# A second level of the seven-product scheme for three of the seven products of an expert's first layer

## The chip, the cores and the metric

The kernel runs on one core of a Trainium2 chip. TensorE (PE) multiplies: a weight load brings in a stationary 128x128 block, and a matmul streams up to 512 columns past it and adds the result up in a bank of PSUM. PSUM has eight banks of 128x512 fp32. VectorE (DVE) and ScalarE (ACT) read and write PSUM and SBUF; GpSimd (POOL) works on SBUF here. SyncE (SP) starts the transfers from and to memory. Each engine runs its own instructions in order and waits for the others by semaphores. The metric is the device time of one execution, in microseconds (us).

## The reference, cut to what matters

```python
x = attention(q, k, v)              # (1152, 512): pooled attention plus attention in a band
# first mixture of experts: 8 experts, P from a softmax and 8 rounds of scaling rows and columns
for e in range(8):
    h = np.maximum(x @ w1[e], 0.0)  # (1152, 512) @ (512, 1024)
    out += P[:, e:e + 1] * (h @ w2[e])          # (1152, 1024) @ (1024, 512)
# second mixture: x is the first one's result; 4 experts, p from an input
for e in range(4):
    h = np.maximum(x @ w1[e], 0.0)
    out += p[:, e:e + 1] * (h @ w2[e])
```

All in fp32. The kernel splits every fp32 operand into a high part and the rest, and makes each product of three matmuls: high by high, high by rest, rest by high.

## The kernel before, in words

The 12 experts run one after the other, each in two groups of 512 hidden columns. A group has two stages. In the first (`quarter_products`, L409, with its matmuls in `product`, L380, on line L396) x times w1 gives the hidden columns; in the second (`tile_products`, L449, matmuls on L455) they are multiplied by w2 for nine tiles of 128 tokens, 12 matmuls of 512 columns each, and `accumulate` (L468) adds the weighted tile to the sum `acc`.

The first stage works on quads: 256 hidden columns of an expert, as 2x2 blocks of 256x128, against x in 2x2 blocks of 576 tokens by 256 inputs. Instead of the eight block products of such a 2x2 product it makes seven, in the order 1, 5, 6, 2, 7, 3, 4, out of sums of blocks (Winograd's form of Strassen's scheme). Every product is done for two halves u of the tokens, 288 columns each: six matmuls (two blocks of 128 inputs, three parts each) into one bank. So a quad is 84 matmuls and a group, with its two quads q, 168. Two groups do without the scheme (`plain_unit`, L372, matmuls on L277): the first of expert 0 and the first of the second mixture, since the sums of x are still being made.

The sums of x (`x_sums`, L866) are made once for each mixture and kept in `sh` and `sl`. The sums of weights are made for each quad (`quad`, L319): POOL subtracts blocks (L327), ACT copies the high part (L301), POOL takes the rest (L303). The results stand in a ring of 12 slots `w1s`, each one block pair for one quad; the raw weights in two buffers `raw1`. The w2 blocks are split in the same way (ring `w2s`). The products come together outside PE: a product is copied from its bank into a `tmp` buffer by ACT (L294), added to a bank's content by DVE into a `tmp` (L406) or to another `tmp` by POOL (L421); other products go on in the bank of an earlier one by PE's own addition. `hidden` (L360) takes the finished block: ACT applies max(.,0) and writes the high part to `ht` (L364), DVE writes the rest (L366), from the bank or from `tmp`.

The order of all instructions is written out beforehand by a planner (`Plan`, L79). It takes the tasks with their assumed durations, walks through time, and gives each engine at each step the task that can begin first, among the next 160 (400 in the attention part) in order of their due times; a due time is the PE clock at which the task was added. Buffers come from rings (`Ring`, L30), in the order in which the program asked for them; a task whose buffer is not free cannot begin. The lists so made are fixed in the program. There are two plans: the attention with the start of expert 0, and all the rest. The scaling rounds of P (`gate_round`, L1023) are mixed into the start of the second plan.

## Time and profile before

| | us |
|---|---|
| median of 3 runs | 1202.19 (1201.57 to 1202.4) |
| the profiled execution | 1204.05 |
| its span, first to last instruction | 1202.3 |
| PE busy in the span | 1191.3 |
| POOL, DVE, ACT busy | 674.2, 664.4, 460.7 |

A line of groups names line, engine, operation, written and read tiles, shape and count; then the busy time of all, the mean of one in ns, and the idle time of the engine ahead of them with what ended it. Matmuls overlap: the duration of one (about 293 ns at 288 columns) is not the time from one to the next, which the chain shows (168 in 22.13 us). A line of the chain has start, length, and what ran. A line of windows has the stretch, its length, and busy time and instructions of PE, PEld (weight loads), DVE, ACT and POOL in it, then the granted clock, DMA share and GB/s.

### The profile page before, as it was taken

The numbers are of one execution on the slowest core, as the hardware profiler recorded it, in microseconds if no ns is written. First come the engines' busy times: TensorE is split into PE (matmuls) and PEld (weight loads), VectorE is DVE, ScalarE is ACT, GpSimd is POOL, SyncE is SP. The second block draws the span as 40 slices with busy tenths as digits, with TensorE's granted clock in tenths as the row PEclk, the third lists the DMA queues.
The fourth block names the chain that finished last, engine by engine and source line by source line (L and its number), as shares of the span: only waits on it lengthen the run. The fifth ranks groups of instructions, "written<-read, shape, count | busy, mean of one in ns | idle before, by whom it ended". The sixth has DMA issues, their size and how long they took to land.

```text
span 1202.3 us, 20145 instructions
## 1 busy us (share of the span) xinstructions
PE 1191.3 (99%) x7800; PEld 1076.9 (90%) x7800; DVE 664.4 (55%) x1208; ACT 460.7 (38%) x1163; POOL 674.2 (56%) x779
## 2 busy tenths in 40 slices
PE   8999999999999999999999999999999999999998
PEld 6889898988989989989989989889899898898997
DVE  6867844635636536546446456367364563653643
ACT  4755451522513514414325325244453252351430
POOL 7968844835836736637538448256384483573620
PEclk9999999999999999999999999999999999999999
DMA  8521210211211201102102112011021121120102
GB/s 215 166 71 36 71 45 27 71 36 36 71 35 36 71 6 66 55 17 71 44 27 71 36 36 71 36 54 35 19 71 37 34 71 36 35 71 22 32 1 79
DMA packets 27344, 63.72 MB, mean 53 GB/s; under 512 B 4528, under 2 KB 5296, under 8 KB 27248
## 3 DMA queue, kind: packets, MB, share of 16 engines
q1 hardware_dynamic: 27248, 62.44, 16.7%
q8 instruction: 61, 1.00, 0.3%
q14 instruction: 35, 0.29, 0.1%
HBM read 60.07 MB, written 2.36 MB: 52 GB/s over the span
## 4 chain that ended last, share of the span: by engine, by line
PE 96%; DMA 1%; POOL 1%; DVE 0%; issue 0%; ACT 0%; SPq 0%; POOLq 0%; DVEq 0%; ACTq 0%
PE bank L455 49%; PE bank L396 40%; PE bank L277 4%; DMA v<-in_v_dram 1%; PE bank L609 0%; PE bank L769 0%; DMA qk<-in_qk_dram 0%; PE bank L931 0%; PE bank L907 0%; PE bank L759 0%; PE bank L734 0%; PE bank L677 0%; PE bank L725 0%; DVE ht L366 0%; POOL t L661 0%
## 5 line engine op out<-in xcount | busy, mean ns | idle before, releaser
L455 PE MATMUL bank<-w2s,ht 128*128 128x512 f32 (+1 forms) x2604 | 595.9, 389 | 0.0
L455 PEld LDWEIGHTS bank<-w2s,ht 128*128 128x128 f32 x2604 | 484.8, 188 | 98.4
L303 POOL TENSOR_TENSOR w2s<-raw,w2s 128x512 fp32r<-128x512 f32 x96 | 132.7, 1392 | 391.1 <-PE bank L455 354.4
L483 DVE SCALAR_TENSOR_TENSOR acc<-bank,prob,acc 128x512 f32<-128x512 f32 (+1 forms) x190 | 142.1, 748 | 323.1 <-PE bank L455 323.1
L396 PE MATMUL bank<-sh,w1s 128*128 128x288 f32 x1408 | 292.8, 294 | 1.4 <-DVE tmp L406 1.4
L396 PEld LDWEIGHTS bank<-sh,w1s 128*128 128x128 f32 x1408 | 229.3, 188 | 1.7 <-DVE tmp L406 1.7
L396 PE MATMUL bank<-xh,w1s 128*128 128x288 f32 x1056 | 226.8, 295 | 0.1
L366 DVE SCALAR_TENSOR_TENSOR ht<-tmp,ht 128x288 fp32r<-128x288 f32 x264 | 216.7, 847 | 4.9 <-ACT ht L364 2.9
L406 DVE TENSOR_TENSOR tmp<-bank,tmp 128x288 f32<-128x288 f32 x352 | 152.9, 450 | 117.2 <-ACT w1s L301 87.7
L396 PE MATMUL bank<-sl,w1s 128*128 128x288 f32 x704 | 205.8, 292 | 0.0
L301 ACT ACTIVATE w2s<-raw 128x512 fp32r<-128x512 f32 x96 | 59.7, 625 | 374.8 <-PE bank L455 364.9
L396 PEld LDWEIGHTS bank<-xh,w1s 128*128 128x128 f32 x1056 | 174.7, 188 | 1.2 <-DVE tmp L406 0.4
L396 PE MATMUL bank<-xl,w1s 128*128 128x288 f32 x528 | 154.5, 293 | 0.0
L303 POOL TENSOR_TENSOR w1s<-t,w1s 128x256 fp32r<-128x256 f32 x176 | 141.4, 804 | 11.6 <-PE bank L396 5.9
L364 ACT ACTIVATE ht<-tmp 128x288 fp32r<-128x288 f32 x264 | 111.8, 444 | 89.9 <-DVE tmp L406 88.7
L303 POOL TENSOR_TENSOR w1s<-raw,w1s 128x256 fp32r<-128x256 f32 x148 | 119.8, 811 | 31.6 <-ACT w1s L301 30.6
L396 PEld LDWEIGHTS bank<-sl,w1s 128*128 128x128 f32 x704 | 132.0, 188 | 0.0
L396 PEld LDWEIGHTS bank<-xl,w1s 128*128 128x128 f32 x528 | 99.1, 188 | 0.9
L294 ACT ACTIVATE tmp<-bank 128x288 f32<-128x288 f32 x176 | 69.4, 409 | 61.1 <-PE bank L396 58.3
L366 DVE SCALAR_TENSOR_TENSOR ht<-bank,ht 128x288 fp32r<-128x288 f32 x120 | 54.4, 456 | 49.4 <-ACT ht L364 49.1
L327 POOL TENSOR_TENSOR t<-raw,t 128x256 f32<-128x256 f32 x88 | 78.1, 887 | 3.1
L421 POOL TENSOR_TENSOR tmp<-tmp,tmp 128x288 f32<-128x288 f32 x88 | 73.9, 858 | 8.6 <-ACT tmp L294 8.6
(112 smaller groups left out, 837.9 us busy)
## 6 DMA issues: line engine op xcount, KB each, us to landing
raw<-in_w1a_dram SPq DMA_DIRECT2D x32, 512.0 KB, 3.5
raw<-in_w2a_dram SPq DMA_DIRECT2D x64, 256.0 KB, 3.3
raw<-in_w1b_dram SPq DMA_DIRECT2D x16, 512.0 KB, 3.5
raw<-in_w2b_dram SPq DMA_DIRECT2D x32, 256.0 KB, 3.1
qk<-in_qk_dram SPq DMA_DIRECT2D x7, 576.0 KB, 7.5
vw<-in_vw_dram SPq DMA_DIRECT2D x8, 320.0 KB, 7.5
v<-in_v_dram SPq DMA_DIRECT2D x8, 288.0 KB
out_dram<-acc SPq DMA_DIRECT2D x8, 256.0 KB, 2.0
```

Of the source, the lines that this page charges most:

```text
L277: nc.tensor.matmul(out=ps[:, 0:U], lhsT=w[:, j, a:a + 128], rhs=b[:, k, c:c + U], start=(k == 0 and p == 0), stop=(k == HP - 1 and p == 2),)
L294: nc.scalar.activation(out=dst(), in_=src(), func=ACTF.Copy, **kw)
L301: plan.add("ACT", copy_cost(n), lambda: nc.scalar.activation(out=b.slot[:, 0], in_=src(), func=ACTF.Copy), (key,), ((b, 0),))
L303: plan.add("POOL", pool_cost(n), lambda: nc.gpsimd.tensor_tensor(out=b.slot[:, 1], in0=src(), in1=b.slot[:, 0].bitcast(F32), op=ALU.subtract),
L327: plan.add("POOL", pool_cost(256), lambda: nc.gpsimd.tensor_tensor(out=t.slot, in0=x(), in1=y(), op=ALU.subtract), (kx, ky), (t,))
L364: plan.add("ACT", c0[0], lambda: nc.scalar.activation(out=ht[:, s, 0, c:c + U], in_=src(), func=ACTF.Relu), (key,), ((*k, 0),))
L366: plan.add("DVE", c0[1], lambda: nc.vector.scalar_tensor_tensor(out=ht[:, s, 1, c:c + U], in0=src(), scalar=0.0, in1=ht[:, s, 0, c:c + U]. ...
L396: nc.tensor.matmul(out=o, lhsT=w.slot[:, j, 128 * k:128 * k + 128], rhs=a, start=(first and k == 0 and n == 0), stop=(k == 1 and n == 2), ...
L406: plan.add("DVE", cost, lambda: nc.vector.tensor_tensor(out=dst.slot, in0=ps.slot[:, 0:U], in1=b.slot, op=ALU.add), (ps, b), (dst,))
L421: plan.add("POOL", pool_cost(U), lambda u=u: nc.gpsimd.tensor_tensor(out=p5[u].slot, in0=p5[u].slot, in1=p1[u].slot, op=ALU.add), (p1[u], ...
L455: nc.tensor.matmul(out=ps.slot[:, 0:nd], lhsT=ht[:, j, a, 128 * n:128 * n + 128], rhs=w[j].slot[:, b, c0:c0 + nd], start=(j == 0 and p == ...
L483: plan.add("DVE", 130 + 1.2 * nd, lambda: nc.vector.scalar_tensor_tensor(out=a, in0=ps.slot[:, 0:nd], scalar=prob[:, n, e:e + 1], in1=a, o ...
```

## The change

- The first stage works on pairs: the two quads of a group together (`pair`, `pair_products`). The weight slots are twice as wide and half as many (6), and one raw buffer holds both quads. What was done twice at 256 columns is done once at 512.
- The products 5, 6 and 1 of a pair get a second level: tokens u by inputs k by quads q is again a 2x2 product, and instead of its eight parts (4 results of 6 matmuls, two parts of three each) seven are made, of three matmuls each. It comes in one by one: with product 5 in the first pair of expert 1, 5 and 6 in the second, all three from expert 2 on; in the second mixture expert 8's second pair has none, and experts 9 to 11 go as 1 to 3 do.
- For it there are, for each such product and pair, three more subtractions of weights on POOL, one more split (ACT and POOL), and, once for each mixture and product, sums of sums of x (`deep_sums`).
- In `deep_first` three of the four result banks start from a copy of another bank, written by ACT into PSUM (`seeded`), and PE goes on adding in them; part 5 goes to a bank of its own, is copied to `tmp`, and DVE adds it in place to two result banks. Where the bank's last PE writer did not cover 288 columns, a matmul of ones goes ahead of the copy (`touched`, `whole`).
- Between the parts stand other PE tasks (`fill`): halves of the last two tiles of the second stage before, the products 2, the products 4.
- The joining of the first level changes: `u2` and `v` are evicted from banks after DVE has added `p1` in the bank, POOL's addition is gone, and three of four `hidden` read a bank. The halves of x in the products 1, 2 and 4 change places.
- The scaling of `acc` by P for expert 0 moves into the middle of the next pair. The logits are made in three matmul groups of 384 columns, and their tile `lg` goes (it borrows three of `acc`).

```diff
-        t = pool.tile([128, 576], F32R, name=f"w1s_{j}")
-        return t[:, 36:548].rearrange("p (a b) -> p a b", a=2)
-    w1s = [w1_slot(big, j) for j in range(8)]
+        t = pool.tile([128, 1088], F32R, name=f"w1s_{j}")
+        return t[:, 36:1060].rearrange("p (a q b) -> p a q b", a=2, q=2)
+    w1s = [w1_slot(big, j) for j in range(4)]
     w2s = [big.tile([128, 2, DM], F32R, name=f"w2s_{j}") for j in range(4)]
     acc = [big.tile([128, DM], F32, name=f"acc_{n}") for n in range(4)]
-    raw1 = [big.tile([128, 4, 256], F32, name="raw1_0")]
+    raw1 = [big.tile([128, 2, 4, 256], F32, name="raw1_0")]
     raw2 = [big.tile([128, DM], F32, name=f"raw2_{j}") for j in range(2)]
...
+    def pair(g, grp, deep):
+        r = load_pair(g, grp)
+        rk = ((r, 0), (r, 1))
+        b11, b21, b12, b22 = (lambda j=BLOCKS.index(k): r.slot[:, :, j] for k in ((0, 0), (1, 0), (0, 1), (1, 1)))
+        def both(src, keys):
+            b = r_w1.new()
+            split(b, lambda: b.slot[:, 0], lambda: b.slot[:, 1], src, keys, 512)
+            return b
+        def minus(out, x, y, keys, key, n):
+            plan.add("POOL", pool_cost(n), lambda: nc.gpsimd.tensor_tensor(
+                out=out(), in0=x(), in1=y(), op=ALU.subtract), keys, (key,))
         def less(x, kx, y, ky):
             t = r_t.new()
-            plan.add("POOL", pool_cost(256), lambda: nc.gpsimd.tensor_tensor(
-                out=t.slot, in0=x(), in1=y(), op=ALU.subtract), (kx, ky), (t,))
-            return lambda: t.slot, t
-        w = {1: split(r_w1, b11, r, 256)}
-        t1, k1 = less(b12, r, b11, r)
-        w[5] = split(r_w1, t1, k1, 256)
-        t2, k2 = less(b22, r, t1, k1)
-        w[6] = split(r_w1, t2, k2, 256)
-        w[2] = split(r_w1, b21, r, 256)
-        t3, k3 = less(b22, r, b12, r)
-        w[7] = split(r_w1, t3, k3, 256)
-        w[3] = split(r_w1, b22, r, 256)
-        t4, k4 = less(b21, r, t2, k2)
-        w[4] = split(r_w1, t4, k4, 256)
+            v = lambda: t.slot.rearrange("p (q b) -> p q b", q=2)
+            minus(v, x, y, (*kx, *ky), t, 512)
+            return v, (t,)
+        def weights(p, src, keys):
+            b = both(src, keys)
+            if p not in deep:
+                return b, None
+            t = r_t.new()
+            v = lambda: t.slot.rearrange("p (i f) -> p i f", i=4)
+            minus(lambda: v()[:, 0:2], lambda: src()[:, 1].rearrange("p (k f) -> p k f", k=2),
+                  lambda: src()[:, :, 0:128], keys, t, 256)
+            minus(lambda: v()[:, 2], lambda: src()[:, 1, 128:256], lambda: v()[:, 0], keys, t, 128)
+            minus(lambda: v()[:, 3], lambda: src()[:, 0, 128:256], lambda: v()[:, 2], keys, t, 128)
+            return b, both(lambda: t.slot.rearrange("p (q b) -> p q b", q=2), (t,))
+        w = {1: weights(1, b11, rk), 2: weights(2, b21, rk)}
+        t1, k1 = less(b12, rk, b11, rk)
+        t2, k2 = less(b22, rk, t1, k1)
+        w[6] = weights(6, t2, k2)
+        w[7] = weights(7, *less(b22, rk, b12, rk))
+        w[4] = weights(4, *less(b21, rk, t2, k2))
+        w[5] = weights(5, t1, k1)
+        w[3] = weights(3, b22, rk)
         return w
...
-    A_OF = {1: ("x", 0, 0), 2: ("x", 0, 2), 4: ("x", 1, 2), 5: ("s", 0), 6: ("s", 1), 7: ("s", 2), 3: ("s", 3)}
+    A_OF = {1: ("x", 1, 0), 2: ("x", 1, 2), 4: ("x", 0, 2), 5: ("s", 0), 6: ("s", 1), 7: ("s", 2), 3: ("s", 3)}
+    DEEP = (5, 6, 1)
...
+    def deep_part(p, w, term, ps, first):
...
+    whole = set()
+    wide = nc.const_aps.tensor(1.0, [128, U], BF16)
+    def touched(ps, n=0):
+        (whole.add if n >= U else whole.discard)(id(ps.slot))
+    def seeded(dst, src):
+        def fn():
+            if id(dst.slot) not in whole:
+                nc.tensor.matmul(out=view(dst), lhsT=row, rhs=wide)
+                touched(dst, U)
+            nc.scalar.activation(out=view(dst), in_=view(src), func=ACTF.Copy)
+        plan.add("ACT", 412.0, fn, (src,), (dst,))
+    def deep_first(p, w, fill):
+        D = {}
+        D[0, 0] = r_bank.new()
+        deep_part(p, w, 1, D[0, 0], True)
+        D[1, 0] = r_bank.new()
+        seeded(D[1, 0], D[0, 0])
+        fill()
+        vb, v = r_bank.new(), r_tmp.new()
+        deep_part(p, w, 5, vb, True)
+        evict(v, vb)
+        deep_part(p, w, 6, D[1, 0], False)
+        D[0, 1] = r_bank.new()
+        seeded(D[0, 1], D[1, 0])
+        fill()
+        deep_part(p, w, 2, D[0, 0], False)
+        deep_part(p, w, 7, D[1, 0], False)
+        D[1, 1] = r_bank.new()
+        seeded(D[1, 1], D[1, 0])
+        add(D[0, 1], D[0, 1], v)
+        fill()
+        deep_part(p, w, 3, D[0, 1], False)
+        add(D[1, 1], D[1, 1], v)
+        deep_part(p, w, 4, D[1, 0], False)
+        fill()
+        return D
+    UQ = ((0, 0), (0, 1), (1, 1), (1, 0))
+    def opening(p, w, fills):
+        fills = list(fills)
+        def fill():
+            if fills:
+                fills.pop(0)()
+        if w[p][1] is not None:
+            D = deep_first(p, w[p], fill)
+        while fills:
+            fill()
+        if w[p][1] is None:
+            D = {}
+            for u, q in UQ:
+                D[u, q] = r_bank.new()
+                product(p, w[p][0], q, D[u, q], u, True)
+        return D
+    def pair_products(w, before, middle=None):
+        X, p1 = opening(1, w, before), {}
+        for u, q in UQ:
+            p1[u, q] = r_tmp.new()
+            evict(p1[u, q], X[u, q])
+        def second_of(u, q):
+            product(2, w[2][0], q, X[u, q], u, False)
+            hidden(lambda: view(X[u, q]), X[u, q], 2 * q, 1, u, P_EVICT)
+        Y, u2, v = opening(6, w, [lambda x=x: second_of(*x) for x in UQ]), {}, {}
+        for u, q in UQ:
+            add(Y[u, q], Y[u, q], p1[u, q])
+            u2[u, q] = r_tmp.new()
+            evict(u2[u, q], Y[u, q])
+        for u, q in UQ:
+            product(7, w[7][0], q, Y[u, q], u, False)
+            v[u, q] = r_tmp.new()
+            evict(v[u, q], Y[u, q])
+        if middle:
+            middle()
+        def fourth_of(u, q):
+            product(4, w[4][0], q, Y[u, q], u, False)
+            hidden(lambda: view(Y[u, q]), Y[u, q], 2 * q, 0, u, P_EVICT)
+        Z = opening(5, w, [lambda x=x: fourth_of(*x) for x in UQ])
+        for u, q in UQ:
+            add(v[u, q], Z[u, q])
+            hidden(lambda b=v[u, q]: b.slot, v[u, q], 2 * q + 1, 0, u, S_EVICT)
+        for u, q in UQ:
+            product(3, w[3][0], q, Z[u, q], u, False)
+            add(Z[u, q], Z[u, q], u2[u, q])
+            hidden(lambda b=Z[u, q]: view(b), Z[u, q], 2 * q + 1, 1, u, P_EVICT)
...
-    r_t = Ring([late.tile([128, 256], F32, name=f"t_{j}") for j in range(3)])
-    r_tmp = Ring([late.tile([128, U], F32, name=f"tmp_{j}") for j in range(8)])
+    r_t = Ring([late.tile([128, 512], F32, name=f"t_{j}") for j in range(4)])
+    r_tmp = Ring([late.tile([128, U], F32, name=f"tmp_{j}") for j in range(9)])
...
+    def deep_sums(p):
+        t = {(u, k): r_tmp.new() for u in range(2) for k in range(2)}
+        for (u, k), d in t.items():
+            hi, lo = part_of(p, k, u)
+            plan.add("POOL", pool_cost(U), lambda d=d, hi=hi, lo=lo: nc.gpsimd.tensor_tensor(
+                out=d.slot, in0=hi.bitcast(F32), in1=lo.bitcast(F32), op=ALU.add), part_keys(p, u), (d,))
...
+        a11, a12, a21, a22 = t[0, 0], t[0, 1], t[1, 0], t[1, 1]
+        two(a22, a21, a22, ALU.add)
+        two(a21, a11, a21, ALU.subtract)
+        two(a11, a22, a11, ALU.subtract)
+        two(a12, a12, a11, ALU.subtract)
+        for i, d in enumerate((a22, a11, a21, a12)):
+            hi, lo = sums[p][i]
+            plan.add("ACT", copy_cost(U), lambda d=d, hi=hi: nc.scalar.activation(
+                out=hi, in_=d.slot, func=ACTF.Copy), (d,), (("l2", p, i, 0),), after=home_keys(p, i))
+            plan.add("DVE", SHARED, lambda d=d, hi=hi, lo=lo: nc.vector.tensor_tensor(
+                out=lo, in0=d.slot, in1=hi.bitcast(F32), op=ALU.subtract),
+                (d, ("l2", p, i, 0)), (("l2", p, i, 1),), after=home_keys(p, i))
...
+    pair_products(pair(0, 1, ()), ())
+    def tiles(g, grp, w, how):
+        fills = []
+        for n in range(NN):
+            if n == 1 and 0 < 2 * (g % E1) + grp <= len(DEEP):
+                deep_sums(DEEP[2 * (g % E1) + grp - 1])
+            fills += tile_fills(g, w, n, how)
+            if n < NN - 2 or (g, grp) == (E1 - 1, 1):
+                while fills:
+                    fills.pop(0)()
...
+                ready = 2 * (g % E1) + grp - 1
+                deep = DEEP[:max(ready, 0)]
+                def middle():
+                    if (g, grp) == (1, 0):
+                        scaled()
+                pair_products(pair(g, grp, deep), rest, middle)
             w2_ = second(g, grp)
             how = "scale" if g == E1 and grp == 0 else "sum"
-            last = g == NE - 1 and grp == 1
+            if (g, grp) != (NE - 1, 1):
+                rest = tiles(g, grp, w2_, how)
```

`deep_part` adds three matmuls of 288 columns for one part, with the wide slot's halves as weights and the x blocks or the second-level sums as columns.

## Rows read from the trace of the kernel before

**Rows 1.** The page, busy times and the granted clock in 40 slices.
```profile
PE 1191.3 (99%) x7800; PEld 1076.9 (90%) x7800; DVE 664.4 (55%) x1208; ACT 460.7 (38%) x1163; POOL 674.2 (56%) x779
PEclk9999999999999999999999999999999999999999
```
**Rows 2.** The chain in order of time: first, middle and last steady pair.
```profile
165.96 22.13 PE bank L396 x168
...
445.64 22.13 PE bank L396 x168
467.77 24.49 PE bank L455 x108
...
1152.25 22.13 PE bank L396 x168
```
**Rows 3.** Waits of PE: who waited for whom, us in total, times, longest.
```profile
PE bank L396 <- DVE tmp L406: 1.4, 1, 1.4
```
**Rows 4.** Windows: the first pair's two stages, then a steady pair's two stages.
```profile
115.35:141.94 26.59, 25.04 (x183) 24.31 (x183) 20.17 (x47) 14.34 (x40) 23.90 (x28) 1.00 0.30 95
141.94:165.96 24.02, 24.02 (x110) 19.84 (x110) 12.36 (x34) 7.84 (x13) 3.84 (x6) 1.00 0.00 1
445.48:467.61 22.13, 22.13 (x170) 22.13 (x169) 15.35 (x29) 14.15 (x37) 20.30 (x24) 1.00 0.30 96
467.61:492.10 24.49, 24.49 (x111) 20.27 (x110) 9.08 (x13) 2.49 (x6) 5.85 (x8) 1.00 0.00 1
```
**Rows 5.** Groups of the page's part 5 and of the list by shape.
```profile
L294 ACT ACTIVATE tmp<-bank 128x288 f32<-128x288 f32 x176 | 69.4, 409 | 61.1 <-PE bank L396 58.3
L301 ACT ACTIVATE w2s<-raw 128x512 fp32r<-128x512 f32 x96 | 59.7, 625 | 374.8 <-PE bank L455 364.9 <-DMA raw<-in_w2a_dram 7.1 <-DMA raw<-in_w2b_dram 1.8
L303 POOL TENSOR_TENSOR w2s<-raw,w2s 128x512 fp32r<-128x512 f32 x96 | 132.7, 1392 | 391.1 <-PE bank L455 354.4 <-ACT w2s L301 36.6
L327 POOL TENSOR_TENSOR t<-raw,t 128x256 f32<-128x256 f32 x88 | 78.1, 887 | 3.1
L406 DVE TENSOR_TENSOR tmp<-bank,tmp 128x288 f32<-128x288 f32 x352 | 152.9, 450 | 117.2 <-ACT w1s L301 87.7 <-PE bank L396 27.1 <-issue 0.2
L790 DVE TENSOR_TENSOR bank<-bank,od 128x288 f32<-128x288 f32 x16 | 6.9, 458 | 8.5 <-PE bank L769 5.6 <-ACT od L777 2.8
L366 DVE SCALAR_TENSOR_TENSOR ht<-tmp,ht 128x288 fp32r<-128x288 f32 x264 | 216.7, 847 | 4.9 <-ACT ht L364 2.9
L366 DVE SCALAR_TENSOR_TENSOR ht<-bank,ht 128x288 fp32r<-128x288 f32 x120 | 54.4, 456 | 49.4 <-ACT ht L364 49.1
L483 DVE SCALAR_TENSOR_TENSOR acc<-bank,prob,acc 128x512 f32<-128x512 f32 x188 | 141.1, 751 | 321.5 <-PE bank L455 321.5
L880 POOL TENSOR_TENSOR tmp<-xh,xl 128x288 f32<-128x288 f32 x32 | 28.1, 903 | 30.5 <-DVE xl L919 19.2 <-ACT xh L795 6.6 <-DVE sl L897 3.4
L897 DVE TENSOR_TENSOR sl<-tmp,sh 128x288 fp32r<-128x288 f32 x32 | 24.4, 792 | 0.5 <-ACT sh L895 0.5
L1064 ACT ACTIVATE acc<-acc,prob 128x512 f32<-128x512 f32 x9 | 6.4, 721 | 16.0 <-DVE acc L480 16.0
```
**Rows 6.** Timeline, steady pair: the last matmuls of product 1, its eviction.
```profile
446.15 0.42 PE L396 MATMUL bank<-xh,w1s 128*128 128x288 f32 x2
446.52 0.41 ACT L294 ACTIVATE tmp<-bank 128x288 f32<-128x288 f32 x1 [1.80 <-PE bank L396]
```
**Rows 7.** Timeline of PE, first pair: where it waited for DVE.
```profile
133.21 0.29 PE L396 MATMUL bank<-xh,w1s 128*128 128x288 f32 x1
134.92 0.40 PE L396 MATMUL bank<-sh,w1s 128*128 128x288 f32 x1 [1.42 <-DVE tmp L406]
```
**Rows 8.** The chain in order of time, first pair: DVE releases PE.
```profile
138.08 0.38 DVE tmp L406
138.46 0.04 issue
138.50 1.86 PE bank L396 x12
```

More of the change, by code (lines that the diff above doesn't have):

```diff
@@ L90, in __init__, with add @@
         self.ranks, self.step = (), None
-    def add(self, eng, cost, fn, reads=(), writes=(), slack=0.0, after=None):
+    def add(self, eng, cost, fn, reads=(), writes=(), slack=0.0, after=()):
         n = len(self.tasks)
@@ L112, in add @@
                 bufs.append(b)
+        for k in after:
+            if k in self.last:
+                deps.add(self.last[k])
+            deps.update(self.readers.get(k, ()))
         deps.discard(n)
@@ new lines, in deep_part, with fn @@
+    def deep_part(p, w, term, ps, first):
+        wb, wt = w
+        s = sums.get(p)
+        b, c = {1: (wb, 0), 2: (wb, 128), 3: (wb, 384), 5: (wt, 0), 7: (wt, 128), 6: (wt, 256), 4: (wt, 384)}[term]
+        if term in (1, 2, 4):
+            u, k = {1: (0, 0), 2: (0, 1), 4: (1, 1)}[term]
+            a, keys = part_of(p, k, u), part_keys(p, u)
+        else:
+            i = {5: 0, 6: 1, 7: 2, 3: 3}[term]
+            a, keys = s[i], [("l2", p, i, hl) for hl in range(2)]
+        def fn():
+            touched(ps, U)
+            for n, (j, hl) in enumerate(PASSES):
+                nc.tensor.matmul(
+                    out=view(ps), lhsT=b.slot[:, j].rearrange("p q b -> p (q b)")[:, c:c + 128], rhs=a[hl],
+                    start=(first and n == 0), stop=(n == 2), skip_group_check=True,
+                )
+        plan.add("PE", 3 * 133.4, fn, [(b, 0, 0), (b, 1, 0), *keys], (ps,))
@@ L876, in x_sums @@
             o = b * S + c
-            keys = [("x", n) for n in range(o // 128, (o + wd - 1) // 128 + 1)]
+            tiles = range(o // 128, (o + wd - 1) // 128 + 1)
             for h in range(2):
@@ new lines, in tile_attention_moe_moe, with own_keys @@
+    sums, homes = {}, {}
+    def own_keys(kind, i=None):
+        return [("l2", p, i_, hl) for (p, i_), (k, j) in homes.items() if k == kind and (i is None or i == j)
+                for hl in range(2)]
+    spare = [([xh[:, k, u * U:u * U + U], xl[:, k, u * U:u * U + U]], "x", u) for k in range(2) for u in range(2)]
+    spare += [([sx[:, j, 0], sx[:, j, 1]], "sx", 0) for j in range(5)]
+    for p in DEEP:
+        kind, i, *_ = A_OF[p]
+        own = (part_of(p, 0, 1), kind, i if kind == "s" else -1)
+        spare.insert(0 if kind == "s" else len(spare), own)
+        sums[p] = []
+        for j in range(4):
+            place, kind, u = spare.pop(0)
+            sums[p].append(place)
+            homes[p, j] = (kind, u)
@@ L905, in fn @@
         def fn():
+            touched(ps)
             for k in range(HP):
@@ L1044, in tile_attention_moe_moe @@
     gate_weights()
-    logits(0)
-    logits(1)
+    for j in range(3):
+        logits(j)
     at = plan.clock
@@ L1058, in tile_attention_moe_moe, with scaled @@
         accumulate(0, n, tile_products(first_w2, n), "copy")
-    for q in (2, 3):
-        quarter_products(quad(0, q), q)
-    w2_ = second(0, 1)
-    for n in range(NN):
-        accumulate(0, n, tile_products(w2_, n), "plain")
-        plan.add("ACT", 625.0, lambda n=n: nc.scalar.activation(
-            out=acc[n], in_=acc[n], func=ACTF.Copy, scale=prob1[:, n, 0:1]),
-            (("prob", 0),), (("acc", n),))
+    pair_products(pair(0, 1, ()), ())
[8 more added lines that the diff above has]
+                    fills.pop(0)()
+            if g == E1 - 1 and grp == 1 and n:
+                turn(n - 1)
+        return fills
+    def scaled():
+        while plan.later:
+            plan.later.pop(0)[1]()
+        for n in range(NN):
+            plan.add("ACT", 625.0, lambda n=n: nc.scalar.activation(
+                out=acc[n], in_=acc[n], func=ACTF.Copy, scale=prob1[:, n, 0:1]),
+                (("prob", 0),), (("acc", n),))
+    rest = tiles(0, 1, second(0, 1), "plain")
     for g in range(1, NE):
```

262 lines of the change are left out of this document (139 added, 123 removed).

## The prediction

> **What bounds the kernel now.** I read the page's busy times first: PE 1191.3 of 1202.3 us, the others about half, and the granted clock full in every slice [rows 1]. The reader is to see there that only less work for PE, or new waits of PE, can move the time much. Then the chain in order of time. From 165.96 us on it is PE alone: 22.13 us for the 168 matmuls of a pair's first stage, 24.49 us for the 108 of its nine tiles, and so on; 21 of the 22 seven-product pairs have this very length, to 0.01 us [rows 2]. So a matmul of 288 columns takes 22.13 / 168 = 131.7 ns of PE, one of 512 takes 24.49 / 108 = 226.8 ns, whichever slots and tiles they read, and a steady pair (46.62 us) holds no wait at all. Of PE's waits on first-stage matmuls one is worth a line, 1.4 us for DVE [rows 3], and it lies in the first pair, whose first stage takes 26.59 us [rows 4, 7]. Last, the windows, for room on the other engines: in a steady first stage POOL is busy 20.30 of 22.13 us, DVE 15.35, ACT 14.15; in the tiles 5.85, 9.08 and 2.49 of 24.49 [rows 4]. POOL at 92% did not hold PE up, since its work is for later.
>
> The change therefore has one thing to gain, PE's matmuls, and one to lose: the unbroken PE stream.
>
> **What it removes from PE.** A product of a pair was 24 matmuls (four units of six). With the second level it is 7 parts of 3, 21. How many products: 1 and 2 in the pairs of expert 1, three in each of the 12 pairs of experts 2 to 7, none in expert 8, 1 and 2 in expert 9, three in the four pairs of experts 10 and 11: 3 + 36 + 3 + 12 = 54, in 20 pairs. 54 x 3 = 162 matmuls x 131.7 ns = **-21.3 us**, all on the path [rows 2]. That I take the same 131.7 ns for groups of three rests on the steady stage, where passing from one product, bank or stage to the next costs nothing. The logits (32 matmuls of 288 columns become 24 of 384) are the same number of columns: 0.
>
> **What it adds on PE.** A matmul of ones ahead of a seed whose bank was last written by something narrow. Narrow writers are the transposes, logits and scaling rounds, and nearly all of these come before the first seeded product or far from one. Bounds: none, or one for each of the 3 x 54 = 162 seeds. I take 2 or 3, at 131.7 ns: **+0.3 us**.
>
> **What it adds as waits.** Each second-level product has three new chains from PE through ACT (and DVE) back to PE. Their lengths: after a product PE is free at 446.28 us (446.15 plus one matmul), and ACT starts its eviction at 446.52: 0.24 us; it takes 0.41 [rows 6]; DVE follows and adds at 0.46; from DVE's end to PE's next matmul it was 0.04 us in one place (138.46 to 138.50) and in the other about 0.40 (the first of three adds from 134.06 ends near 134.52, PE starts at 134.92) [rows 7, 8]. The trace has no ACT copy into PSUM. Its nearest rows are ACT from bank to `tmp`, 0.409, and DVE, whose add takes 0.450 into `tmp` and 0.458 into a bank [rows 5]; so 0.41 from both sides, nothing gained.
> - Part 1, copy, part 6: 0.24 + 0.41 + 0.04 to 0.40 = 0.69 to 1.05 us. In between stand a filler and part 5: 0.79 + 0.395 = 1.19 us where the filler is a product of six, 1.36 + 0.395 = 1.75 where it is half a tile (6 x 0.2268). Margin 0.14 to 0.50, or 0.70 to 1.06.
> - Part 6, copy, DVE's add, part 3: 1.18 to 1.54 us against filler, part 2, part 7, filler: 2.37. Margin 0.8 or more.
> - Part 7, copy, add, the bank's next user: the same 1.18 to 1.54 against filler, parts 3 and 4, filler: 2.37.
>
> Only the first margin is thin, and only where the filler is a product: in products 6 and 5, 18 + 20 = 38 times. The waiting part has the rest of PE's list behind it, the tiles at its end. What can be late is ACT, which does the copy in order. Its work for a pair: 10 weight splits and 4 of w2 at 0.625, 16 halves of `ht`, 12 evictions, 9 seeds and 3 evictions of part 5 at 0.41: 8.8 + 16.4 = 25.2 us, where it was 14.15 + 2.49 = 16.6 [rows 4, 5]. Within first stage and two tiles of fillers (159 x 0.1317 + 5.44 = 26.4 us) some 19 to 21 us of it fall: 72 to 81% busy, against 64% now. One split of 0.625 ahead of a copy makes it late by 0.625 - 0.50 to 0.625 - 0.14, so up to 0.5 us: 38 x 0.5 = 19 us at the far end, 0 at the near. I choose near the row that resembles it most, the steady stage with ACT at 64% and no wait: 0.05 us each, **+2 us**. PE's list can also take another filler first, if the planner saw the lateness coming.
>
> **What else is added, at nothing.** POOL per pair: 14 splits at 1.39, 4 differences at 512 columns (1.39 to 1.77), for each of three products a difference at 256 (0.89) and two at half of that: 30.4 to 31.9 us where it was 26.2, of a pair's new 45.4 [rows 4, 5]. The tiles' 24.49 us, in which POOL is now 76% idle, hide it. The single raw buffer lets the next load go only when the last split of a pair is through; the next pair's first weights are wanted a whole stage of tiles later. If that cover were gone, PE would wait for one weight's chain, 0.89 + 0.89 + 0.63 + 1.39 = 3.8 us, once a pair. DVE per pair: 18 adds at 0.45, 12 halves of `ht` from banks at 0.456 and 4 from `tmp` at 0.847, 9 tiles at 0.751: 23.8 us, where it was 24.4 [rows 4, 5]. The second-level sums of x, six times 4 POOL operations of 0.90, 8 on DVE of 0.79 or less, 4 on ACT, lie among tiles; uncovered, DVE's 6.3 us would show six times. Scaling `acc` for expert 0 is nine ACT operations of 0.72 as before, now within a pair that has only one seeded product: 0.
>
> **What it may give besides.** In the first pair PE stood still twice, from 133.34 to 134.92 and from 138.20 to 138.50, 1.9 us, behind DVE, busy 20.17 of 26.59 us there [rows 4, 7, 8]. The new joining takes 4 adds and 8 x (0.847 - 0.456) off DVE, 4.9 us. Bounds: nothing to -1.9; I take **-1 us**. A loss is as open as this gain, since the attention's order is planned anew with wider slots; it is in the range.
>
> Sum: -21.3 + 0.3 + 2 - 1 = -20.0. The profiled execution took 1204.05 us (span 1202.3 and 1.75 around it): 1184.05. The median is 1.86 lower: **1182.2 us**.
>
> **A rule that speaks against it.** No row here shows what PE does with a bank that ACT has filled. The Trainium skill, "PSUM — Partial Sum Buffer", section "The four PSUM rules", says that ACT and DVE writes leave the bits alone that decide between adding and overwriting, that a seed is safe either way only as zero, and that any other should go through PE. By the rule followed to the letter every seed costs a matmul, and the sum would be -21.3 + 21.3 = 0; the code needs it only after a narrow writer, since the bits stay set. That is the third rival.
>
> **The rivals.**
> - *ACT's copies come late, a little.* PE waits 0.1 to 0.35 us for each second-level product. For it: the thin margin, ACT's load, splits of weights that carry earlier due times than the copies. Against: zero waits now with 64% and 69% busy engines. Time: 54 x 0.2 = 11 us: 1182.2 - 2 + 11 = about **1191**.
> - *The fillers are spent early and the copies stand bare: slower.* PE's list takes the fillers while it waits for the first copy, and then has only parts 5, 2 and 7 between. Uncovered: 0.69 to 1.05 less 0.395, and 1.18 to 1.54 less 0.79: 0.7 to 1.4 us a product. It decides from 0.395 us on, where a product's wait eats its three matmuls. At 0.8: 54 x 0.8 = 43: about **1224**. For it: eight banks, of which four hold one product, up to four the next and one part 5, so that order is forced. Against: four fillers for each product, 3.2 to 5.4 us, against three chains of 3.1 to 4.1 us in all.
> - *It does not save what it says*: nearly every seed with its own matmul of ones: -21.3 + 21.3 - 1 + 2: about **1203**. Against: all matmuls of both stages are 288 or 512 columns wide.
>
> **How the numbers follow.** Forecast, 1177 to 1187: 0.66. Late copies, 1187 to 1199.8: 0.20. Even, by seeds or by waits that just eat the gain: 0.04. Slower: 0.08. Below 1177, if the start gains more: 0.02. Within 0.2% is 1199.8 to 1204.6, about what can be told from no change. Faster 0.88, same 0.04, slower 0.08. The range 1177 to 1195 holds the first case and most of the second, 0.81.
>
> **What would show it.** 162 matmuls of 288 columns fewer, some 3534 instead of 3696 in products and parts; first stages of the full pairs of 159 x 131.7 ns = 20.9 us net of fillers; a steady pair of 45.4 us; few or no PE waits for ACT; ACT copies from bank to bank near 0.41 us. I am wrong if a steady pair shows PE waits of over 0.4 us for ACT or DVE, if the matmuls of ones number more than ten, or if the spacing of 131.7 ns changes with groups of three.

## The result, and the profile after

| | before | after |
|---|---|---|
| median of 4 runs each on one chip, us | 1202.30 (1201.57 to 1205.83) | 1183.86 (1182.57 to 1184.74) |
| profiled execution, us | 1204.05 | 1184.74 |
| its span, us | 1202.3 | 1183.0 |

The ratio is 0.984, 95% interval 0.9818 to 0.9862: 18.4 us faster by the medians, 1.7 us from the forecast of 1182.2. A second execution with a profile (run a0_again below) gave 1182.71.

The page of the changed kernel, busy times (compare [rows 1]):

```profile
PE 1174.2 (99%) x7630; PEld 1057.5 (89%) x7630; DVE 666.7 (56%) x1275; ACT 575.8 (49%) x1391; POOL 715.2 (60%) x689
```

PE lost 17.1 us of busy time and 170 matmuls: 162 of the products and 8 of the logits. The granted clock was 1.000 of full speed over the span, as before. ACT gained 115 us of work, POOL 41; in the steady pairs PE waits for neither.

Groups of the list by shape (compare [rows 5]); lines of the new kernel are L297 for the old L294, L403 for L366, L459 for L406, L303 and L305 for L301 and L303, L444 and L481 for the products and the parts, L602 for the tiles:

```profile
L297 ACT ACTIVATE tmp<-bank 128x288 f32<-128x288 f32 x318 | 124.3, 412 | 82.6 <-PE bank L481 45.2 <-PE bank L444 27.8 <-DVE bank L459 7.0
L500 ACT ACTIVATE bank<-bank 128x288 f32<-128x288 f32 x162 | 64.2, 396 | 161.0 <-PE bank L481 160.9
L403 DVE SCALAR_TENSOR_TENSOR ht<-tmp,ht 128x288 fp32r<-128x288 f32 x88 | 84.0, 991 | 0.0
L1107 DVE TENSOR_TENSOR tmp<-tmp,tmp 128x288 f32<-128x288 f32 x24 | 26.6, 1108 | 0.5
L674 PE MATMUL bank<-const-bfloat16-1.0 128*128 128x128 bf16 x132 | 12.2, 259 | 0.8 <-PEq L1407 0.8
```

L500 is the seed: 162 copies of 0.396 us from bank to bank. L674, the scaling rounds, is the only line that multiplies by ones, 132 times as before: no seed needed a matmul of its own.

PE's waits in the whole span (who waited for whom, us, times, longest; compare [rows 3]) are all in the attention and the scaling rounds, and none is on a product (L444), a part (L481) or a tile (L602). No weight load (PEld) of a product or a part waits either. The largest:

```profile
PE bank L898 <- POOL ed L867: 1.3, 2, 0.8
```

The chain in order of time, one steady pair (start, us, what; compare [rows 2]). Seven tiles come first as one piece of 84 matmuls, then the parts in threes, with the halves of the last two tiles (L602 x6) and the products 2 and 4 (L444) between:

```profile
277.88 19.04 PE bank L602 x84
296.92 0.39 PE bank L481 x3
297.31 1.37 PE bank L602 x6
298.68 0.79 PE bank L481 x6
...
303.85 1.38 PE bank L602 x6
...
305.63 0.79 PE bank L444 x6
...
323.48 19.04 PE bank L602 x84
```

There is no piece of another engine in it, and the next pair begins 45.60 us after this one, as do all twelve pairs from expert 2 to expert 7 (tiles at 232.28, 277.88, ... 779.48). Before it was 46.62.

Windows (columns as in [rows 4]): the first pair's two stages, then a steady pair, cut into its products with two tiles and its seven other tiles:

```profile
115.49:140.38 24.89, 24.76 (x183) 24.16 (x183) 18.77 (x45) 14.65 (x35) 17.24 (x16) 1.00 0.18 64
140.38:164.34 23.96, 23.96 (x111) 19.82 (x110) 16.88 (x43) 6.70 (x13) 6.21 (x7) 1.00 0.08 23
297.07:323.48 26.41, 26.41 (x183) 25.37 (x183) 14.03 (x29) 19.12 (x47) 12.81 (x12) 1.00 0.17 60
323.48:342.52 19.04, 19.04 (x86) 15.77 (x86) 8.49 (x15) 3.34 (x7) 15.61 (x16) 1.00 0.10 28
```

The first pair, which has no second level, took 24.89 us for its first stage where it took 26.59, with the same 168 matmuls: PE's two stops behind DVE [rows 7, 8] are gone but for 0.13 us. In the steady products ACT is busy 72%, POOL only 49%: half of its work in a pair now lies in the tiles.

**Where the gain comes from.** Both chains are one unbroken order of work from the first long tile piece of expert 0 to the last tile, so lengths between like points can be taken apart. Before:

```profile
74.73 8.38 PE bank L455 x36
...
234.70 24.49 PE bank L455 x108
...
1174.37 24.65 PE bank L455 x120
```

After:

```profile
74.91 8.38 PE bank L602 x36
...
1156.40 23.31 PE bank L602 x114
```

From 74.73 to 1199.02 it was 1124.29 us, from 74.91 to 1179.71 it is 1104.80: -19.49. The other profiled execution gives -19.51 (72.91 to 1177.69), although its attention part began the same piece 2.0 us earlier: in these two executions the written-out part repeats to hundredths, and what scatters is the start. The 162 matmuls are -21.33 at 131.7 ns, expert 0's pair -1.80 (74.73 to 165.96 before, 74.91 to 164.34 after), and the rest is **+3.6 us**, which I look for below: 0.4 in expert 1, 2.05 in the twelve steady pairs (-12.16 where 36 products of 3 matmuls make -14.2; **0.17 us a pair**), 1.2 from there to the end.

### The profile page after: what moved, and what is told of

Same layout as the page of the kernel before. It is cut to its first block, busy times and chain, and to the rows that moved or that the text cites. A ratio compares the mean times of both kernels' runs of the same rounds, so it can differ in the third digit from the quotient of the medians.

```text
span 1183.0 us, 19706 instructions
## 1 busy us (share of the span) xinstructions
PE 1174.2 (99%) x7630; PEld 1057.5 (89%) x7630; DVE 666.7 (56%) x1275; ACT 575.8 (49%) x1391; POOL 715.2 (60%) x689
## 4 chain that ended last, share of the span: by engine, by line
PE 97%; DMA 2%; DVE 0%; POOL 0%; SPq 0%; issue 0%; ACT 0%; POOLq 0%
PE bank L602 50%; PE bank L444 27%; PE bank L481 13%; PE bank L280 4%; DMA v<-in_v_dram 2%; PE bank L773 0%; PE bank L933 0%; PE bank L1154 0%; PE bank L1130 0%; PE bank L923 0%; PE bank L898 0%; PE bank L841 0%; PE bank L889 0%; POOL t L825 0%; PE bank L674 0%; PE bank L766 0%
## 5 line engine op out<-in xcount | busy, mean ns | idle before, releaser
L602 PE MATMUL bank<-w2s,ht 128*128 128x512 f32 (+1 forms) x2604 | 608.5, 389 | 0.1
L602 PEld LDWEIGHTS bank<-w2s,ht 128*128 128x128 f32 x2604 | 481.1, 188 | 94.6 <-DVE ht L403 0.6
L305 POOL TENSOR_TENSOR w1s<-t,w1s 128x512 fp32r<-128x512 f32 x142 | 190.9, 1351 | 220.0 <-ACT w1s L303 198.3
L403 DVE SCALAR_TENSOR_TENSOR ht<-bank,ht 128x288 fp32r<-128x288 f32 x296 | 129.4, 449 | 157.9 <-ACT ht L401 157.1
L444 PE MATMUL bank<-xh,w1s 128*128 128x288 f32 x800 | 184.4, 294 | 0.0
L401 ACT ACTIVATE ht<-bank 128x288 fp32r<-128x288 f32 x296 | 119.1, 410 | 116.3 <-DVE bank L459 60.0
L444 PE MATMUL bank<-sh,w1s 128*128 128x288 f32 x800 | 170.0, 295 | 0.0
L297 ACT ACTIVATE tmp<-bank 128x288 f32<-128x288 f32 x318 | 124.3, 412 | 82.6 <-PE bank L481 45.2
L459 DVE TENSOR_TENSOR bank<-bank,tmp 128x288 f32<-128x288 f32 x284 | 125.1, 460 | 68.0 <-ACT bank L500 55.0
L305 POOL TENSOR_TENSOR w2s<-raw,w2s 128x512 fp32r<-128x512 f32 x96 | 124.6, 1311 | 48.9 <-PE bank L602 26.4
L500 ACT ACTIVATE bank<-bank 128x288 f32<-128x288 f32 x162 | 64.2, 396 | 161.0 <-PE bank L481 160.9
L344 POOL TENSOR_TENSOR t<-raw 128x512 f32<-128x512 f32 (+1 forms) x60 | 72.8, 1213 | 110.9 <-DMA raw<-in_w1a_dram 73.8
L444 PEld LDWEIGHTS bank<-xh,w1s 128*128 128x128 f32 x800 | 137.4, 188 | 0.2
L444 PEld LDWEIGHTS bank<-sh,w1s 128*128 128x128 f32 x800 | 132.2, 188 | 0.3
L303 ACT ACTIVATE w1s<-t 128x512 fp32r<-128x512 f32 x142 | 89.2, 628 | 69.6 <-POOL t L344 68.4
L444 PE MATMUL bank<-xl,w1s 128*128 128x288 f32 x400 | 118.2, 295 | 0.0
L444 PE MATMUL bank<-sl,w1s 128*128 128x288 f32 x400 | 118.1, 295 | 0.0
L305 POOL TENSOR_TENSOR w1s<-raw,w1s 128x512 fp32r<-128x512 f32 (+1 forms) x82 | 101.3, 1241 | 15.8 <-ACT w1s L303 7.9
L481 PE MATMUL bank<-sh,w1s 128*128 128x288 f32 x304 | 85.1, 295 | 0.0
L403 DVE SCALAR_TENSOR_TENSOR ht<-tmp,ht 128x288 fp32r<-128x288 f32 x88 | 84.0, 991 | 0.0
L481 PE MATMUL bank<-xh,w1s 128*128 128x288 f32 x284 | 79.8, 296 | 0.0
```

The lines of the kernel that those rows point to most:

```text
L297: nc.scalar.activation(out=dst(), in_=src(), func=ACTF.Copy, **kw)
L303: plan.add("ACT", copy_cost(n), lambda: nc.scalar.activation(out=hi(), in_=src(), func=ACTF.Copy), keys, ((b, 0, part),))
L305: plan.add("POOL", pool_cost(n), lambda: nc.gpsimd.tensor_tensor(out=lo(), in0=src(), in1=hi().bitcast(F32), op=ALU.subtract), (*keys, (b, ...
L344: plan.add("POOL", pool_cost(n), lambda: nc.gpsimd.tensor_tensor(out=out(), in0=x(), in1=y(), op=ALU.subtract), keys, (key,))
L401: plan.add("ACT", c0[0], lambda: nc.scalar.activation(out=ht[:, s, 0, c:c + U], in_=src(), func=ACTF.Relu), (key,), ((*k, 0),))
L403: plan.add("DVE", c0[1], lambda: nc.vector.scalar_tensor_tensor(out=ht[:, s, 1, c:c + U], in0=src(), scalar=0.0, in1=ht[:, s, 0, c:c + U]. ...
```

## Experiments

My theory: the gain is PE's 162 matmuls and nothing else, and it is kept because a filler (another PE task) stands in PE's list before each part that needs a seed. Rivals: the gain is from the new joining and order (e1); the fillers don't matter (e2); the margin is wider, or narrower, than I worked out (e5, e11); ACT's other work can break it (e9).

**e1, no second level.** All else stays: the pairs, the wide slots, the joining, the order in which the program adds its tasks. The planner makes its lists anew, as in e2, e4, e6 to e8 and e10.

```diff
-    DEEP = (5, 6, 1)
+    DEEP = ()
```

> The change without its second level: all products of a pair at one level of 24 matmuls, with the new pairs, the new joining and the new order kept. Theory A (the whole gain is 162 matmuls of 131.7 ns, and PE never waits for what stands in their place): a steady pair is back at 46.6 to 46.7 us, the time at 1201 to 1204 us. Theory B (the new joining, which takes work off DVE, and the relief of the start give a good part of it): half of the gain stays, about 1193 us.

Measured: 1203.76 against 1203.41, ratio 1.0005 (0.9982 to 1.0028), as theory A said. A steady pair is 46.68 us, 0.06 over before: so the new joining and order cost 0.06 of the 0.17, and without the second level no gain is left. One part of the account is not as it looks, though: expert 0's pair, which has no second level in either kernel, gains only 0.88 us here (73.67 to 164.02), and 0.69 in e6, not 1.80. DVE's operations come in the same order there as in the changed kernel, but two of `ht` from `tmp` (L403) take 3.01 us (from 134.80) where the changed kernel's take 1.37 (from 136.74), and PE waits behind them. From e1's chain and from its waits:

```profile
134.88 2.93 DVE ht L403 x2
...
138.24 1.85 PE bank L444 x12
```

```profile
PE bank L444 <- DVE tmp L459: 0.9, 1, 0.9
```

So about 0.9 us of the 1.80 goes with the length of these two operations, and not with the new joining.

**e4, product 5 alone.**

```diff
-    DEEP = (5, 6, 1)
+    DEEP = (5,)
```

> Only product 5 gets the second level, in 20 pairs. Theory A (each second-level product is worth its three matmuls, 0.395 us, less about 0.04 for the changes between parts): a steady pair, 46.68 us without any, goes to 46.3 to 46.35; the profiled span near 1195. Rival, a fixed gain or loss that comes with the first seeded product (banks, order): not between the span without (1201.8) and with three (1183.0) by the number of products.

Measured, in one execution: span 1193.2 (1194.99 in all); a steady pair is 46.355 (tiles at 231.59, 277.94): 0.325 below e1's, where three products give 46.68 - 45.60 = 1.08, or 0.36 each. The gain goes nearly in proportion; of the 0.395 of three matmuls a product keeps eight to nine tenths.

**e2, fillers ahead.** In `opening` the fillers go before the second level's parts.

```diff
+        while fills:
+            fill()
         if w[p][1] is not None:
             D = deep_first(p, w[p], fill)
-        while fills:
-            fill()
```

> The fillers (halves of the last two tiles, the products 2 and 4) all stand ahead of the seven parts instead of between them; the work is the same. Theory A (the fillers hide the chains from PE through ACT and DVE back): PE waits 0.3 to 0.65 us for the first copy and 0.4 to 0.75 us for the copy and the add of each of the 54 products, 38 to 75 us in all: 1222 to 1259 us, with these waits in the trace under ACT's copy from bank to bank and DVE's add. Theory C (the copies are quick enough, the fillers cover nothing that matters): 1182 to 1188 us.

Measured: 1232.22, ratio 1.0252 (1.0209 to 1.0295): slower than before, within theory A's range. A steady pair is 48.09, 0.83 us more for each second-level product. The chain of this kernel in product 1 shows what was hidden, and under it stand the waits of PE's weight loads (PEld) for seeds in the whole span:

```profile
305.48 0.41 PE bank L481 x3
305.89 0.02 issue
305.92 0.41 ACT bank L500
306.32 0.04 issue
306.36 0.68 PE bank L481 x3
```

```profile
PEld bank L481 <- ACT bank L500: 30.2, 73, 0.8
```

Here a seed stands bare between two parts. That is not so for all: the planner makes new lists, and 73 of the 162 seeds hold PE up. Products also wait 8.4 us for evictions into `tmp`, and some copies begin late behind splits of weights. The fillers are what the change lives on; the slower rival of the prediction was in the main this mechanism, at this price (0.7 to 1.4 us a product, 0.8 taken), in a kernel whose order allows it.

**e5, the margin.** Each seed's copy is made three times in a row.

```diff
-            nc.scalar.activation(out=view(dst), in_=view(src), func=ACTF.Copy)
+            for _ in range(3):
+                nc.scalar.activation(out=view(dst), in_=view(src), func=ACTF.Copy)
```

> ACT makes each copy from bank to bank three times, so that each of the three chains of a product is 0.8 us longer; the order of the engines stays as it is. Theory A with a thin first margin (0.14 to 0.50 us where the filler is a product): PE waits 0.3 to 0.65 us in 38 products and hardly elsewhere: 11 to 25 us, 1195 to 1209 us. Rival, ACT is what bounds the stage (its whole load matters, not the chain): all 162 copies show, 0.8 us each less what margins take: over 1227 us. Rival, the margins are wide everywhere: under 1188 us.

Measured: 1226.65, ratio 1.0205 (1.0187 to 1.0224). That is far above theory A's 1195 to 1209, and so near the 1227 of the rival in which ACT's whole load bounds that the time can't exclude it; e11 does. A steady pair is 47.89, 2.29 over the changed kernel. The chain of this kernel in product 6, and the waits of PE's weight loads in its whole span:

```profile
312.67 0.40 ACT bank L501
313.08 0.02 issue
313.10 0.40 ACT bank L501
313.50 0.02 issue
313.53 0.40 ACT bank L501
313.93 0.04 issue
313.98 0.68 PE bank L481 x3
```

```profile
PEld bank L481 <- ACT bank L501: 37.8, 92, 0.6
```

In a steady pair the weight loads wait five times: 0.56, 0.38 and 0.38 us in the three chains of product 6, and 0.38 and 0.37 in the second and third of product 5. The first chain of product 5 is free, since the planner has put product 7 behind its part 1; in the first of product 6 the copy also begins late, behind other work of ACT. Matmuls go on more slowly after such a wait, so that it costs about 0.42 us in all (315.27 to 316.48 for six matmuls of 0.79), the 0.56 about 0.6: together the 2.29. I had the second and third chain at a margin of 0.8 or more (the margin is the time by which a copy can be later before PE waits), since their copies are needed a filler and two parts later. But the copy into `D[0, 1]` reads `D[1, 0]`, and part 7 writes `D[1, 0]`; the copy into `D[1, 1]` reads it too, and part 4 writes it. So PE must wait for the copy to have *read*, one filler and one part after its source was finished, just as in the first chain. Where the fillers are products all three margins are the same: 1.19 us against about 0.73 (0.24 until ACT starts [rows 6], the copy, and 0.02 to 0.04 on either side).

**e11, the copy twice.** The edit is against e5.

```diff
-            for _ in range(3):
+            for _ in range(2):
```

> Each copy from bank to bank twice instead of three times. With three copies (0.82 us longer) PE waited 0.38 to 0.44 us in each of the three chains of products 6 and 5; so the margin should be about 0.42 us in all three, and with two copies (0.42 longer) PE should wait 0.05 us or less in each: a steady pair of 45.6 to 45.9 us, a span of 1183 to 1189. If the waits came from ACT's load as a whole, half of the 2.29 us a pair should stay: 46.7.

Measured, in one execution: span 1182.6 (1184.4 in all), steady pairs 45.60 to 45.66, no wait on a part. One more copy (0.42 with its start) fits, two more (0.84) make 0.38 of wait: the margin lies between 0.42 and 0.46, and ACT's 54 us of further work in the span cost next to nothing by themselves. The rival of e5 is out.

**e9, ACT's other work.** The copy of the high part in every weight split is made twice; the planner doesn't know it.

```diff
-        plan.add("ACT", copy_cost(n), lambda: nc.scalar.activation(
-            out=hi(), in_=src(), func=ACTF.Copy), keys, ((b, 0, part),))
+        def high():
+            for _ in range(2):
+                nc.scalar.activation(out=hi(), in_=src(), func=ACTF.Copy)
+
+        plan.add("ACT", copy_cost(n), high, keys, ((b, 0, part),))
```

> ACT makes the high part of every split of weights twice, 14 operations of 0.63 us more in a pair, with the order of all engines as it is; the chains of the copies are as short as before, only ACT's queue ahead of them is longer. Theory D (what the chains can bear is a lateness of ACT of about 0.4 us, and splits stand ahead of copies at the start of products 6 and 1): PE waits 0.5 to 1.5 us in each pair, 1193 to 1215 us. Rival, ACT is under half busy and swallows it: 1183 to 1188 us.

Measured: 1240.46, ratio 1.0313 (1.0285 to 1.0341), beyond the 1193 to 1215 of theory D: a miss in size. A steady pair is 48.27, 2.67 more. ACT is busy 758.6 us, 61%. The two largest waits of PE in this kernel, the first for seeds, the second for evictions into `tmp`:

```profile
PE bank L484 <- ACT bank L503: 22.7, 17, 1.4
PE bank L447 <- ACT tmp L297: 15.1, 20, 1.2
```

And its chain where splits stand ahead of an eviction (L305 is the split, L297 the copy out of a bank into `tmp`):

```profile
367.68 0.64 ACT w1s L305
...
368.35 1.17 ACT w1s L305 x2
...
369.54 0.63 ACT w1s L305
370.17 0.30 ACT ht L404
370.47 0.31 ACT tmp L297
370.78 0.04 issue
370.82 3.46 PE bank L447 x24
```

With ACT 61% busy over the span the profiled execution is 55 us longer. Late copies were a real rival: two doubled splits in a row are 2.4 us, more than the margin of a seed. The 17 waits for seeds, 1.3 us each, lie within the 0.5 to 1.5 us a pair of theory D; the evictions, which it did not name, make the rest. In the changed kernel the planner places the splits around the copies, with durations that hold (0.625 planned, 0.628 measured).

**e3, a matmul of ones ahead of every seed.**

```diff
-            if id(dst.slot) not in whole:
-                nc.tensor.matmul(out=view(dst), lhsT=row, rhs=wide)
-                touched(dst, U)
+            nc.tensor.matmul(out=view(dst), lhsT=row, rhs=wide)
+            touched(dst, U)
```

> Every seed gets its own matmul of ones ahead of it, 162 more matmuls of 288 columns in bf16; nothing else changes. Theory A (a matmul of 288 columns costs its 131.7 ns wherever it stands): plus 21.3 us, and up to 7 us more where the copy, which now has to wait for it, comes late for part 6: 1205 to 1213 us, the gain is gone. Rival: such a matmul slips into a gap between the parts: 1184 to 1195 us.

Measured: 1247.21, ratio 1.0387 (1.0347 to 1.0427): a miss, and the slowest of all. A steady pair is 49.13, 0.39 us more for each of nine seeds on the average, three times the matmul's own 0.13. The chain of this kernel and its waits:

```profile
325.26 0.15 PE bank L497
325.41 0.02 issue
325.43 0.40 ACT bank L499
325.84 0.04 issue
325.88 0.67 PE bank L481 x3
```

```profile
PEld bank L481 <- ACT bank L499: 34.8, 108, 0.3
```

The matmul of ones (L497) is written out when the copy is, behind the filler in PE's list, and the copy can start only after it. So in six of the nine chains of a pair (108 of 162) the cover is lost too. A matmul of ones written ahead of the filler was not tried.

**e6 and e7, the 0.17 us a pair.** Both without the second level (compare e1's 46.68). In e6 products 7 and 3 are lists of 12 matmuls that change between two banks at each; in e7 the fillers stand between the four units of the opening products, so that matmuls of 512 and 288 columns alternate in sixes.

```diff
+                for n, (j, hl) in enumerate(PASSES):
+                    for u, q in two:
+                        touched(D[u, q], U)
+                        nc.tensor.matmul(
+                            out=view(D[u, q]), lhsT=w.slot[:, j, q, 128 * k:128 * k + 128],
...
```

> No second level. The products 7 and 3 of two units run as one list of 12 matmuls that goes from one bank to the other with every matmul, 40 changes of bank more in a pair; work, columns and weights are the same. If a change of the output bank is what makes the matmuls of the parts a little dearer (about 0.01 us for each group of three), a steady pair rises from 46.68 to 46.9 to 47.1 us. If not, it stays at 46.68.

```diff
             for u, q in UQ:
                 D[u, q] = r_bank.new()
                 product(p, w[p][0], q, D[u, q], u, True)
+                fill()
+        while fills:
+            fill()
```

> No second level. The halves of the last two tiles stand between the four units of product 1, the products 2 and 4 between those of 6 and 5. If passing between groups of 512 and 288 columns costs 0.02 to 0.04 us each way in and out, as the pieces of the changed kernel's chain let one think, a steady pair rises from 46.68 to about 46.8 us; if only the groups of three cost, it stays at 46.68. No PE waits either way.

Measured, one execution each: in e6 the pairs without a wait are 46.68 to 46.70 (tiles at 328.86, 375.56, 422.26, 468.94), so a change of bank at every matmul costs 0.02 us in a pair at most; the span, 1206.9, is longer for waits on DVE of up to 0.9 us in other pairs. In e7 a pair is 46.72: +0.04 for mixing, less than the 0.1 that I had for it. With e1's 0.06, about 0.07 of the 0.17 is left to the groups of three and to the tile halves among them. The pieces of the changed kernel's own pair (277.88 to 323.48) put the weight on the tile halves: the four take 5.54 us, where 24 x 226.8 ns is 5.44, and the 21 groups of three 8.35, where 63 x 131.7 ns is 8.30. The two accounts agree only roughly; what makes it I leave open.

**e8, e10: the sums of sums earlier.** The second level can begin sooner if the sums of x are ready sooner. In e8 this is done in both mixtures (60 second-level products instead of 54), in e10 in the second one only (59: products 5 and 6 from expert 8's second pair on, all three from expert 9's first). The line `MADE` is e10's; e8 has `(1, 0): ((1, 6), (4, 1))` and nothing at `(1, 1)`.

```diff
-            if n == 1 and 0 < 2 * (g % E1) + grp <= len(DEEP):
-                deep_sums(DEEP[2 * (g % E1) + grp - 1])
+            for at, p in MADE.get((g, grp), ()):
+                if n == at:
+                    deep_sums(p)
...
-                ready = 2 * (g % E1) + grp - 1
-                deep = DEEP[:max(ready, 0)]
+                deep = [p for x, ps in MADE.items() for _, p in ps
+                        if x < (g, grp) and (x[0] < E1) == (g < E1)]
...
+    MADE = {(0, 1): ((1, 5),), (1, 0): ((1, 6),), (1, 1): ((1, 1),), (E1, 0): ((1, 5), (4, 6)), (E1, 1): ((1, 1),)}
```

> The sums of sums of x are made sooner: in the first mixture those of 5, then 6 and 1 together; in the second those of 5 and 6 in the first group's tiles, then 1. That is 6 more second-level products, 60 instead of 54. Theory A: 6 x 0.36 = 2.1 us less, 1181 to 1183 us where the changed kernel had 1183.9, a ratio to the kernel before near 0.9825. Rival: DVE, which makes them at up to 1.1 us an operation, comes late with them or with the tiles' sums in those groups, and PE waits: 1183 to 1190 us.

> The changed kernel as it is, beside the next one on the same chip: 1182 to 1186 us, a ratio to the kernel before of 0.983 to 0.986.

> Sums of sums as the changed kernel makes them in the first mixture, sooner in the second alone: those of 5 and 6 in the tiles of expert 8's first group, those of 1 in its second. 5 more second-level products than the changed kernel. Theory A: DVE has room there (6.4 of 24.5 us busy among those tiles before), so no wait of PE and 5 x 0.36 = 1.8 us less than the changed kernel on the same chip, in the chain from the start of the second mixture to its end above all. Rival: DVE late as it was in expert 1's pair when it made two in one stage: 1 us or more of it comes back as a wait.

Measured: e8 1181.51, ratio 0.9832 (0.9807 to 0.9857); its chain (71.39 to 1175.16) is 1.03 us shorter than the changed kernel's, half of the 2.1 that six products should bring. So the time lies in theory A's range, but the rival's mechanism is there too: around the tiles of expert 1's first group, where the early sums of sums are made, the chain runs through DVE for 27 us (181.38 to 208.30), and at its end a part's weights wait 1.1 us for a DVE add. Then, on one chip, the changed kernel again: 1183.51, ratio 0.9837 (0.9811 to 0.9863), and e10: 1181.06, ratio 0.9816 (0.9791 to 0.984). The intervals overlap, so the timings alone don't separate them. The chains do. e10's, from the second mixture's plain pair on:

```profile
808.79 22.13 PE bank L280 x168
...
1151.98 23.31 PE bank L602 x114
```

The changed kernel's on the same chip:

```profile
809.33 22.14 PE bank L280 x168
...
1154.38 23.31 PE bank L602 x114
```

343.19 against 345.05 us: -1.86, where five products at e4's 0.36 make -1.8. By this e10 is the version to keep.

## Why the prediction was right

- **The matmuls, -21.3:** right in number (162) and in effect; e1 and e4 show that the gain is theirs and nearly in proportion. 131.7 ns holds for groups of three to within 0.01 us a group.
- **Ones, +0.3:** none was needed, as the count of L674 shows. My bounds were 0 and 162 matmuls; I took 2 or 3. A matmul of ones ahead of every seed costs not the 21 us at which I priced it, but 63 where e3 puts it (1247.21 - 1183.86), since it takes away cover too. The Trainium skill ("PSUM — Partial Sum Buffer", section "The four PSUM rules") advises to put any seed other than zero through PE, or to add it after the bank has been read out. The Trainium skill says in the same section that a matmul that doesn't open a group adds to data which ACT wrote wherever an earlier matmul has left the bit set. The trace agrees as far as it goes: it has 162 seeds that are copies of partial sums, and no matmul of ones for them (L674); the bits themselves no row shows.
- **Waits, +2:** there were none, and yet 3.6 us are missing. The sentence that failed is "passing from one product, bank or stage to the next costs nothing", and a steady pair is 45.60 us, not 45.4. A change of bank does cost nothing that e6 can show, but mixing long and short matmuls (e7, 0.04 a pair), the new joining and order (e1, 0.06) and what is left at the groups of three and the tile halves among them (0.07) add up to 0.17 us in each of some 20 pairs. The size came near by chance; the cause was another.
- **Margins:** 0.14 to 0.50 for the first chain was right near its upper end (0.42 to 0.46, e5 and e11): the delay from ACT to PE is 0.04, as in [rows 8], and not the 0.40 that I had as the other bound. "0.8 or more" for the second and third was wrong: I counted who reads the seeded bank, and not who next writes the bank that the seed is read from. So I had 38 thin places; in e5 92 weight loads wait.
- **The first pair, -1:** -1.8, near the end of my bounds (-1.9), and in part luck: the same joining gave -0.9 in e1.
- **Loads of a steady pair:** over 277.88 to 323.48 DVE was busy 22.63, ACT 22.46 and POOL 28.41 us; forecast 23.8, 25.2, 30.4 to 31.9. That is 50, 49 and 62% of a pair, and no weight came late. DVE's `ht` from `tmp` takes 0.991 where I had 0.847, and its sums of sums 1.108 where I had 0.79 or less; both lie in cover.
- **Late copies, 0.20:** did not happen, but e9 shows that lateness of ACT would have cost more than the 0.1 to 0.35 us a product that I gave it (2.67 a pair, 0.9 a product) once splits bunch, on evictions as well as on copies.

The sum, -21.3 + 0.3 + 2 - 1 = -20.0, became -21.3 + 0 + 3.6 - 1.8 = -19.5. The mechanism of the main term was right; that the sum came within 0.5 is in part luck, since the misses of the small terms (-0.3, +1.6, -0.8) nearly cancel.

## What to carry to other kernels

When a chain through another engine is put into a full stream of TensorE, write down for each link both who reads the new result and who next overwrites its source: the shorter of the two is the margin, and other work placed inside it decides whether the edit pays (here 18 us faster, 29 slower with the fillers moved). An average load says little about lateness: ACT at 61% went with 55 us of loss where its other work stood in bunches ahead of the copies, and at 53% with none (e11). When the removed matmuls are the gain, take something off it for each rearranged stage even where no wait shows; here it was 0.17 us a pair, a sixth of what the three products bring.

## What the runs showed of the hardware that was not expected

- ACT copies 128x288 fp32 from bank to bank in 0.396 us, from bank to SBUF in 0.412 (162 and 318 copies).
- PE's next matmul starts 0.04 us after the ACT copy that it waits for has ended (chains of e2, e3, e5 and e9), or the DVE add ([rows 8]). The first group of three behind it took 0.50 us to the next group (e5, 313.98 to 314.48) instead of 0.395.
- DVE's operations with both operands in SBUF vary from kernel to kernel: `ht` from `tmp` took 0.847 us before, 0.991 after, and 0.655 in e9, while from a bank it was 0.456, 0.449 and 0.452. The timelines point to POOL: of those `ht` from `tmp` that stand alone there (before, after, e1, e9), the 12 during which POOL ran nothing all took 0.45 to 0.46 us, and the 215 beside a POOL operation 0.44 to 1.55. No run was made to test it.
